# mLSTM cell and SwiGLU block on one core: another order of engines and transfers ahead of the first hidden block

## The chip, the core and the metric

The kernel runs on one core of one Trainium2 chip. The metric is the device time of one execution in microseconds. The times are medians of several executions of the same program; single executions of it lie between 551.8 and 552.71 us.

## What is computed

The reference is an mLSTM cell over 4 batches, 8 heads, 768 steps and a head size of 40, then a gated feed-forward block over the 3072 resulting tokens of width 320, with 1536 hidden features.

```python
for t in range(S):
    m_new = np.maximum(f_gate[:, :, t] + m, i_gate[:, :, t])
    f_stab = np.exp(f_gate[:, :, t] + m - m_new)
    i_stab = np.exp(i_gate[:, :, t] - m_new)
    m = m_new
    C = f_stab * C + i_stab * outer(vt, kt)
    n = f_stab * n + i_stab * kt
    denom = np.maximum(np.abs(n . qt), 1.0)
    y[:, :, t] = sigmoid(o_gate[:, :, t]) * (C @ qt) / denom
x = y.transpose(0, 2, 1, 3).reshape(3072, 320)
g = x @ w_gate
out = (g * sigmoid(g) * (x @ w_val)) @ w_out
```

## The kernel before, in words

The sequence is cut into six chunks g of 128 steps; a chunk holds the same 128 steps of all four batches, that is 512 tokens. For each chunk the cell is computed in matrix form (scores of q and k, weighed by decays, times v, plus the contribution of the state), and the result is turned so that features lie on partitions (xT). The feed-forward block of the chunk follows: `hidden(g, m)` makes one of 12 blocks of 128 hidden features with 20 matmuls (L651, gate rows on the partitions 0 to 63 and value rows on 64 to 127, side by side), a Silu (L656) and a product (L657); `project` multiplies the 12 blocks with w_out (L667, L674). While the block of chunk g runs on PE, the cell of chunk g + 1 is put between its matmuls by hand-written tables (`slots`, `after`, `ahead`). The schedule is manual: every engine does its instructions in the order in which the code emits them, and waits are added where data or rooms need them.

Before the first `hidden` nothing can be put between, so the first chunk has functions of its own (`first_...`), in an order written out by hand at the end of that part. In that order:

- `first_mask`, `first_inputs`, `first_maxima` and `first_exp` make the decay weights W0 of the first chunk, which lie in `h_sb[:, 0:8]`, the room that later holds hidden blocks. Each batch u has two of the eight places.
- `first_turn(P, ...)` turns k and q of two batches (P is 0 for batches 0 and 1, and 1 for 2 and 3) with whole 128x128 transposes (L509) and copies the results. `turn_one` (L296), which later chunks use, does it with 64-row pieces, two side by side.
- `first_scores(P)` multiplies k and q (L519) and puts the products into W0 (L523, DVE). `first_own(u)` multiplies W0 with v (L530), which reads W0 of batch u. `first_x(u)` divides (L535 to L538, DVE). `first_gate(P)` multiplies with the sigmoid of o_gate (L544, DVE) and copies 64 columns (L545, POOL). `sig(P)` is that sigmoid (L463, ACT).
- `first_seam(P, engs)` turns x to xT (L564) and copies it with the three named engines. `first_state(P)` makes the state (L552), `first_kept` copies it.
- `burn(n)` is n matmuls of no use, which keep PE busy.

The weights come as 8-byte floats. `piece_load(p)` asks for a piece (L165): for gate and value weights two transfers, gate rows to partitions 0 to 63 on SP's queue, value rows to 64 to 127 on ACT's queue for the first pieces and on SP's for later ones; for w_out one transfer on SP's queue. A piece lands in a room of its own (`raw`, two in turn) or in a tile that is still free (`home`: parts of `h_sb`, `wo_sb`). Then `scale(j)` splits block j on ACT (L190 the upper words, L192 the lower), `join(j)` shifts and masks the upper words on DVE (L199, L200), and `rounded(j)` adds the lower ones (L207, on POOL, or on DVE where the code names it). `convert` is the three together. Piece 0 holds block 0, piece 1 block 1, pieces 2 to 6 two blocks each, pieces 7 to 9 w_out.

ACT and SP ask for transfers in the same order in which their other instructions stand. A transfer request that must wait for a room holds everything behind it on that engine. SP has no other work: it asks for k, q and v of both P (L117), then o_gate of P = 0, o_gate of P = 1, and then the gate halves.

PSUM has eight banks in two groups of four, "cell" and "gen"; `bank(name, tag)` takes the next of its group in turn and waits until what it held was read.

Of the kernel before, what the change touches and what calls it, by code (L numbers as in the profile page):

```python
# [19 lines left out]
SUB = 64  # L20
# [4 lines left out]
def kernel(  # L25
# [112 lines left out]
    PIECES = [("gv", 0, 1), ("gv", 1, 1)] + [("gv", m, 2) for m in range(2, NFC, 2)] + [("o", m, 4) for m in range(0, NFC, 4)]  # L138

    def piece_load(p, home=None):  # L140
        kind, m, n = PIECES[p]
        if kind == "gv":
            a, d = NKC, n * 128
            src = [(slice(i * HP, (i + 1) * HP), w[:, m * 128:(m + n) * 128].rearrange("(c p) f -> p c f", p=HP))
                   for i, w in enumerate((moe_w_gate, moe_w_val))]
            queues = (nc.sync, nc.scalar if p < 5 else nc.sync)
        else:
            a, d = n, DM
            src = [(slice(0, 128), moe_w_out[m * 128:(m + n) * 128].rearrange("(a p) d -> p a d", p=128))]
            queues = (nc.sync,)  # L150
# [8 lines left out]
        if home is None:  # L159
            raw = conv.tile([128, 4 * NKC * 128], U32, name="raw")  # L160
        else:
            raw = home.rearrange("p a t -> p (a t)").bitcast(U32)
# [22 lines left out]
    def scale(j):  # L185
        if j in blocks:
            lo, hi, dst = blocks[j]
            a, d = hi.shape[1], hi.shape[2]
            top = conv.tile([128, NKC * 128], F32, name="top", bufs=1).rearrange("p (a d) -> p a d", a=a)
            nc.scalar.mul(top, hi.bitcast(F32), 2.0 ** -112)  # L190
            low = conv.tile([128, NKC * 128], I32, name="low").rearrange("p (a d) -> p a d", a=a)
            nc.scalar.mul(low, lo, 2.0 ** -29)  # L192
            blocks[j] = (low, top.bitcast(U32), dst)
# [97 lines left out]
    def turn_one(P, src, dst, engs):  # L291
        tp = [bank("tp_kq").rearrange("p (a t) -> p a t", t=SUB) for _ in range(2)]
        for a in range(UA):
            h = P * UH + 2 * a
            for i in range(2):
                nc.tensor.transpose(tp[i][:, a, :], src[half(i), h:h + 2, :].rearrange("p h d -> p (h d)"),  # L296
                                    ident[half(i), half(i)])
        for i in range(2):
            copy(engs[i], dst[:, P * UA:(P + 1) * UA, half(i)], tp[i])
# [128 lines left out]
    def xT(n):  # L428
        return xTs[max(n - 1, 0) % 2]
# [44 lines left out]
    A, V, G = nc.scalar, nc.vector, nc.gpsimd  # L474
    HH = H // 2
# [65 lines left out]
    def first_gate(P):  # L541
        for u in (2 * P, 2 * P + 1):
            x = x_sb[:, u, 0:DM].rearrange("p (h d) -> p h d", d=D)
            nc.vector.tensor_tensor(x, x, o_sb[:, u * H:(u + 1) * H], op=ALU.mult)  # L544
# [13 lines left out]
    def first_seam(P, engs):  # L558
        for c, eng in zip(range(0, NKC, 2), engs):
# [5 lines left out]
            copy(eng, xT(0)[:, c:c + len(cs), 2 * P * L:(2 * P + 2) * L].rearrange("p c (u s) -> p c u s", u=2), tp)  # L565

# [13 lines left out]
    first_turn(1, k_sb, kT, (A, A))  # L580
    first_x(0)
    first_turn(1, q_sb, qT, (A, V))
    load(o_sb, o_gate, 0, 1)
    piece_load(0)
# [5 lines left out]
    piece_load(1)  # L590
    burn(3)
    first_own(2)
    piece_load(2, h_sb[:, 1:1 + NKC])
# [3 lines left out]
    first_gate(0)  # L597
    first_x(2)
    first_x(3)
    first_gate(1)  # L600
    first_seam(0, (A, A, V))
    scale(0)
    ps1 = first_state(1, "gen")
    burn(1, "gen")
    piece_load(3, h_sb[:, NH - NKC:])
    join(0)
    first_seam(1, (A, A, V))
    rounded(0, V)
    first_kept(0, first_state(0), A)
    first_kept(1, ps1, V)  # L610
    convert(1, V)
    nc.scalar.activation(warm, warm, AF.Silu)
    piece_load(4, wo_sb)
    piece_load(5)

# [104 lines left out]
    def load_all(dst, a, n):  # L720
        for P in range(2):
            load(dst, a, n, P)

    run = lambda f, *a, **b: (lambda: f(*a, **b))
# [9 lines left out]
        1: [run(piece_load, 6), run(late_decay)],  # L734
# [4 lines left out]
        6: [run(turn, 1, (A, A), (A, V)), run(piece_load, 7)],  # L739
        7: [run(weights_sub, 1, 0), run(weights_mask, 0), run(weights_sub, 1, 1), run(weights_mask, 1), run(nc.gpsimd.memset, q_sb, 0.0)],  # L740
        8: [run(weights_exp, 0), run(weights_exp, 1), run(weigh_values, G, 0), run(weigh_values, G, 1),
            run(piece_load, 8)],
        9: [run(do_scores), run(do_weigh, 0), run(do_weigh, 1), run(do_decayed, 2), run(load_all, o_sb, o_gate, 1)],
        10: [run(do_add, 1), run(do_state, 2), run(rounded, 12), run(load_squares, q_sq, q, 2, (0,))],
        11: [run(do_attend, 1, 0), run(do_gather, 1, 0, False), run(piece_load, 9),
# [107 lines left out]
```

## Time and profile before

| what | value |
|---|---|
| median of three runs | 551.9 us (551.8 to 552.71) |
| the profiled execution's own time | 551.99 us |
| its span, from first to last instruction | 550.0 us |
| PE busy | 544.9 us |
| DVE busy | 236.1 us |
| ACT busy | 136.1 us |
| POOL busy | 103.0 us |
| HBM read | 35.68 MB |
| granted PE clock | 1.00 throughout |

A line of the timeline gives the start in us from the span's start, the duration in us, the engine (a q behind it means that the engine's sequencer asks for a transfer), the line of the kernel, the operation, the tiles written and read, and how many instructions were merged; in brackets stands the idle time before it and what ended it. A line of the chain gives start, duration, engine, tile and line of that piece of the chain that ended last. A line of the transfers gives the tiles, the queue, the number of requests, their size and the median time from request to landing. Times in words of the text are us from the span's start.

### The profile page before, as it was taken

What the parts mean: (1) busy time and instruction counts of PE and PEld (TensorE: products, weight loads), DVE (VectorE), ACT (ScalarE), POOL (GpSimd) and SP (SyncE); (2) the same over time, 40 slices, a digit from 0 to 9 for tenths busy, and PEclk for the clock granted to TensorE, in tenths of its full rate; (3) what the DMA queues carried; (4) which work ended last, traced back from release to release, by engine and by line L of the source; (5) the groups of instructions that cost most, each with busy time, mean ns of one, the idle gap of its engine ahead of it and who ended that gap; (6) DMA issues with size and microseconds to landing.
All of it is one profiled execution on the core that took longest, in us unless ns stands there. A gap on an engine that the chain in (4) does not pass through costs nothing.

```text
span 550.0 us, 11592 instructions
## 1 busy us (share of the span) xinstructions
PE 544.9 (99%) x4989; PEld 311.4 (57%) x4989; DVE 236.1 (43%) x397; ACT 136.1 (25%) x203; POOL 103.0 (19%) x95
## 2 busy tenths in 40 slices
PE   8999999999999999999999999999999999999997
PEld 4964556774555575545575545576455567444475
DVE  5778668961346232455421545531436621111100
ACT  4376755352110133011024101115110100111100
POOL 2304265673011060011133011124001100000000
PEclk9999999999999999999999999999999999999999
DMA  9999997878431762660564551395000131000000
GB/s 123 177 294 184 188 277 154 146 104 118 53 49 23 120 112 64 74 74 11 87 117 104 63 72 14 59 146 113 1 1 2 32 63 40 12 1 0 2 24 24
DMA packets 223994, 45.69 MB, mean 83 GB/s; under 512 B 214504, under 2 KB 219112, under 8 KB 223944
## 3 DMA queue, kind: packets, MB, share of 16 engines
q1 hardware_dynamic: 222036, 42.11, 46.7%
q10 hardware_dynamic: 1908, 2.85, 1.9%
q8 instruction: 39, 0.64, 0.5%
q14 instruction: 11, 0.09, 0.1%
HBM read 35.68 MB, written 4.01 MB: 72 GB/s over the span
## 4 chain that ended last, share of the span: by engine, by line
PE 98%; DVE 1%; ACT 0%; issue 0%; ACTq 0%; DVEq 0%
PE gv_ps L651 57%; PE o_ps L667 24%; PE o_ps L674 5%; PE inter L377 2%; PE sp L331 2%; PE intra L382 2%; PE add L353 1%; PE first_y L530 1%; PE burn L469 1%; PE tp_kq L509 1%; PE sp L519 1%; PE wps L480 0%; PE tp_kq L296 0%; PE wps L484 0%; PE wps L489 0%; PE tp_x L439 0%
## 5 line engine op out<-in xcount | busy, mean ns | idle before, releaser
L651 PE MATMUL gv_ps<-xT,wgv_sb 64*128 64x512 f32 x1440 | 316.6, 593 | 0.3 <-DVE wgv_sb L207 0.3
L651 PEld LDWEIGHTS gv_ps<-xT,wgv_sb 64*128 64x128 f32 x1440 | 138.1, 187 | 159.1 <-issue 156.4
L657 DVE TENSOR_TENSOR h_sb<-sg,gv_ps 128x512 f32<-128x512 f32 x72 | 49.5, 688 | 212.3 <-ACT sg L656 212.3
L667 PE MATMUL o_ps<-wo_sb,h_sb 128*128 128x320 f32 x480 | 130.5, 433 | 0.0
L667 PEld LDWEIGHTS o_ps<-wo_sb,h_sb 128*128 128x128 f32 x480 | 90.8, 190 | 41.0 <-issue 3.8
L656 ACT ACTIVATE sg<-gv_ps 128x512 f32<-128x512 f32 x72 | 43.0, 597 | 263.7 <-PE gv_ps L651 263.7
L456 POOL TENSOR_SCALAR_AFFINE_SELECT w_sb<-w_sb 64x1024 f32<-64x1024 f32 x20 | 28.5, 1423 | 63.9 <-DVE w_sb L451 62.9
L362 POOL TENSOR_TENSOR C<-C,dec 128x328 f32<-128x328 f32 x20 | 14.5, 738 | 134.8 <-DVE C L369 134.8
L661 ACT COPY z_sb<-o_ps 128x320 f32<-128x320 f32 x24 | 10.0, 423 | 93.2 <-PE o_ps L667 89.4
L403 POOL TENSOR_TENSOR o_sb<-o_sb,y_sb 128x640 f32<-128x640 f32 x10 | 14.2, 1431 | 78.9 <-DVE y_sb L394 78.9
L674 PE MATMUL o_ps<-wo_sb,h_sb 128*128 128x320 f32 x96 | 26.9, 437 | 0.0
L451 DVE TENSOR_TENSOR w_sb<-g_T,w_sb 128x1024 f32<-128x1024 f32 x10 | 13.1, 1354 | 28.6 <-DMA w_sb<-M_dram 28.6
L426 DVE STREAM_TRANSPOSE xT<-x_sq 128x640 f32<-128x640 f32 x16 | 12.5, 822 | 22.9 <-DMA x_sq<-x_sb 22.9
L674 PEld LDWEIGHTS o_ps<-wo_sb,h_sb 128*128 128x128 f32 x96 | 17.9, 190 | 7.2
L394 DVE TENSOR_TENSOR y_sb<-y_sb,intra 64x328 f32<-64x328 f32 x40 | 19.7, 492 | 0.7
L369 DVE TENSOR_TENSOR C<-C,add 40x328 f32<-40x328 f32 (+1 forms) x36 | 17.7, 493 | 1.2 <-POOL C L362 0.6
L377 PEld LDWEIGHTS inter<-C,qT 64*64 64x64 f32 x640 | 10.2, 134 | 7.3 <-issue 6.1
L460 ACT ACTIVATE w_sb<-w_sb 128x1024 f32<-128x1024 f32 x10 | 10.6, 1058 | 12.7 <-POOL w_sb L456 12.7
L207 POOL TENSOR_TENSOR wgv_sb<-wgv_sb,low 128x640 int32<-128x640 int32 x6 | 9.3, 1546 | 23.5 <-DVE wgv_sb L200 23.5
L341 POOL TENSOR_TENSOR vw_sb<-v_sb,w_sb 128x656 f32<-128x656 f32 x10 | 12.8, 1306 | 0.4
L338 DVE TENSOR_TENSOR w_sb<-sp,w_sb 128x512 f32<-128x512 f32 x20 | 12.7, 682 | 0.0
L397 DVE TENSOR_SCALAR den<-den 128x16 f32<-128x16 f32 x10 | 12.2, 1215 | 0.3
(132 smaller groups left out, 344.5 us busy)
## 6 DMA issues: line engine op xcount, KB each, us to landing
w_sb<-M_dram SPq DMA_DIRECT2D x10, 512.0 KB, 7.3
x_sq<-x_sb SPq DMA_DIRECT2D x128, 40.0 KB, 2.0
k_sb<-in_k_dram SPq DMA_DIRECT2D x12, 320.0 KB, 6.0
v_sb<-in_v_dram SPq DMA_DIRECT2D x12, 320.0 KB, 5.6
o_sb<-in_o_gate_dram SPq DMA_DIRECT2D x12, 320.0 KB, 5.5
raw<-in_moe_w_out_dram SPq DMA_DIRECT2D x3, 1280.0 KB, 7.5
out_dram<-z_sb SPq DMA_DIRECT2D x24, 160.0 KB, 1.8
q_sb<-in_q_dram SPq DMA_DIRECT2D x32, 64.0 KB, 2.3
```

The source lines that it names most:

```text
L362: nc.gpsimd.tensor_tensor(state(s + 1)[:, a], state(s)[:, a], dec[:, s - 2, a].unsqueeze(2).to_broadcast([128, UA, D1]), op=ALU.mult)
L369: nc.vector.tensor_tensor(c, c, ps[r], op=ALU.add)
L377: nc.tensor.matmul(inter[two][half(i), a, :], lhsT=qT[half(two), P * UA + a, half(i)], rhs=state(2 * n + i)[half(two), P * UA + a, :], sta ...
L394: nc.vector.tensor_tensor(t, t, intra[i][half(c)], op=ALU.add)
L403: eng.tensor_tensor(o, o, y[:, :, 0:D], op=ALU.mult)
L451: nc.vector.tensor_tensor(w_sb[:, heads(P)], gb, w_sb[:, heads(P)], op=ALU.subtract)
L456: nc.gpsimd.affine_select(w, w, compare_op=ALU.is_ge, fill=NEG, base=0, pattern=[[0, UH], [1, SUB]], channel_multiplier=-1)
L651: nc.tensor.matmul(ps[i], lhsT=wgv_sb[half(i), m, PAIRS[kc][i] if g < 2 else kc, :], rhs=x[half(i), kc, :], start=(kc == 0), stop=(kc == N ...
L656: nc.scalar.activation(sg, ps[0], AF.Silu)
L657: nc.vector.tensor_tensor(hid(g, m), sg, ps[1], op=ALU.mult)
L667: nc.tensor.matmul(p, lhsT=hid(g, m)[:, ts(u, L)], rhs=wo_sb[:, m, :], start=(m == 0), stop=(m == NFC - 1))
L674: nc.tensor.matmul(ps[u], lhsT=hid(g, m)[:, ts(u, L)], rhs=wo_sb[:, m, :], start=(m == 0), stop=(m == NFC - 1))
```

## The change

The change touches only the part ahead of the first `hidden`, the list of pieces, and the slots in which later pieces are asked for.

- Pieces: blocks 0 to 3 become one piece each, blocks 4 to 11 pairs; so pieces are numbered one higher from there on. Value halves go on ACT's queue up to piece 5 instead of up to piece 4.
- Rooms: piece 2 (block 2) lands in `h_sb[:, 2:5]`, piece 3 (block 3) in `h_sb[:, 8:11]`, piece 4 in `wo_sb`, piece 7 in `h_sb[:, 8:13]`.
- The second turn of k and q is done by `turn_one`, k's in "gen" banks, and `first_x(0)` stands behind both turns instead of between them.
- Piece 0 is asked for ahead of the second half of o_gate, piece 1 behind it; pieces 2 and 3 directly one behind the other ahead of `sig(1)`.
- `scale(0)` and `join(0)` move ahead of `sig(1)` and behind `first_x(2)`; `rounded(0, V)` moves ahead of `first_seam(1)`.
- `first_gate(0)` is done by POOL. One `burn` of three goes.
- `scale(1)` stands ahead of `first_kept(0)`; `join(1)` and `rounded(1, V)` behind `first_kept(1)`.
- `scale` is written as two functions; `first_seam` gets an argument `between` that stays empty.

```diff
--- before.py
+++ after.py
@@ -135,7 +135,7 @@
 
 
     raws = {}
-    PIECES = [("gv", 0, 1), ("gv", 1, 1)] + [("gv", m, 2) for m in range(2, NFC, 2)] + [("o", m, 4) for m in range(0, NFC, 4)]
+    PIECES = [("gv", m, 1) for m in range(4)] + [("gv", m, 2) for m in range(4, NFC, 2)] + [("o", m, 4) for m in range(0, NFC, 4)]
 
     def piece_load(p, home=None):
         kind, m, n = PIECES[p]
@@ -143,7 +143,7 @@
             a, d = NKC, n * 128
             src = [(slice(i * HP, (i + 1) * HP), w[:, m * 128:(m + n) * 128].rearrange("(c p) f -> p c f", p=HP))
                    for i, w in enumerate((moe_w_gate, moe_w_val))]
-            queues = (nc.sync, nc.scalar if p < 5 else nc.sync)
+            queues = (nc.sync, nc.scalar if p < 6 else nc.sync)
         else:
             a, d = n, DM
             src = [(slice(0, 128), moe_w_out[m * 128:(m + n) * 128].rearrange("(a p) d -> p a d", p=128))]
@@ -159,7 +159,7 @@
         if home is None:
             raw = conv.tile([128, 4 * NKC * 128], U32, name="raw")
         else:
-            raw = home.rearrange("p a t -> p (a t)").bitcast(U32)
+            raw = flat(home).bitcast(U32)
         raw = raw[:, 0:2 * a * d]
         for (r, w), queue in zip(src, queues):
             queue.dma_start(out=raw[r].rearrange("p (a d) -> p a d", a=a), in_=w.bitcast(U32))
@@ -182,15 +182,25 @@
                 for c in range(0, n, 2):
                     blocks[NFC + (m + c) // 2] = (lo[:, c:c + 2], hi[:, c:c + 2], wo_sb[:, m + c:m + c + 2, :])
 
-    def scale(j):
+    def scale_top(j):
         if j in blocks:
             lo, hi, dst = blocks[j]
             a, d = hi.shape[1], hi.shape[2]
             top = conv.tile([128, NKC * 128], F32, name="top", bufs=1).rearrange("p (a d) -> p a d", a=a)
             nc.scalar.mul(top, hi.bitcast(F32), 2.0 ** -112)
+            blocks[j] = (lo, top.bitcast(U32), dst)
+
+    def scale_low(j):
+        if j in blocks:
+            lo, *rest = blocks[j]
+            a, d = lo.shape[1], lo.shape[2]
             low = conv.tile([128, NKC * 128], I32, name="low").rearrange("p (a d) -> p a d", a=a)
             nc.scalar.mul(low, lo, 2.0 ** -29)
-            blocks[j] = (low, top.bitcast(U32), dst)
+            blocks[j] = (low, *rest)
+
+    def scale(j):
+        scale_top(j)
+        scale_low(j)
 
     def join(j):
         if j in blocks:
@@ -288,8 +298,8 @@
     M_dram = tc.dram_tile([BH, S - L], F32, name="M_dram")
 
 
-    def turn_one(P, src, dst, engs):
-        tp = [bank("tp_kq").rearrange("p (a t) -> p a t", t=SUB) for _ in range(2)]
+    def turn_one(P, src, dst, engs, tag="cell"):
+        tp = [bank("tp_kq", tag).rearrange("p (a t) -> p a t", t=SUB) for _ in range(2)]
         for a in range(UA):
             h = P * UH + 2 * a
             for i in range(2):
@@ -472,6 +482,7 @@
         return slice(u * BH, (u + 1) * BH)
 
     A, V, G = nc.scalar, nc.vector, nc.gpsimd
+    run = lambda f, *a, **b: (lambda: f(*a, **b))
     HH = H // 2
     wps = {}
 
@@ -538,10 +549,10 @@
         nc.vector.tensor_tensor(x_sb[:, u, 0:DM].rearrange("p (h d) -> p h d", d=D), y[:, :, 0:D],
                                 den.to_broadcast([128, H, D]), op=ALU.mult)
 
-    def first_gate(P):
+    def first_gate(P, eng):
         for u in (2 * P, 2 * P + 1):
             x = x_sb[:, u, 0:DM].rearrange("p (h d) -> p h d", d=D)
-            nc.vector.tensor_tensor(x, x, o_sb[:, u * H:(u + 1) * H], op=ALU.mult)
+            eng.tensor_tensor(x, x, o_sb[:, u * H:(u + 1) * H], op=ALU.mult)
         nc.gpsimd.tensor_copy(x_sb[:, 2 * P:2 * P + 2, DM:], x_sb[:, 2 * P:2 * P + 2, 0:HP])
 
     def first_state(P, tag="cell"):
@@ -555,7 +566,7 @@
     def first_kept(P, ps, eng):
         copy(eng, state(2)[:, P * UA:(P + 1) * UA], ps)
 
-    def first_seam(P, engs):
+    def first_seam(P, engs, between={}):
         for c, eng in zip(range(0, NKC, 2), engs):
             cs = range(c, min(c + 2, NKC))
             tp = bank("tp_x")[:, 0:len(cs) * 2 * L].rearrange("p (c u s) -> p c u s", u=2, s=L)
@@ -563,6 +574,8 @@
                 for b in range(2):
                     nc.tensor.transpose(tp[:, w - c, b, :], x_sb[:, 2 * P + b, ds(PAIRS[w][0] * HP, 2 * HP)], ident)
             copy(eng, xT(0)[:, c:c + len(cs), 2 * P * L:(2 * P + 2) * L].rearrange("p c (u s) -> p c u s", u=2), tp)
+            for f in between.get(c, ()):
+                f()
 
     burn(7)
     banks = [(u, j) for j in range(2) for u in range(B)]
@@ -577,41 +590,45 @@
     first_scores(0)
     first_own(0)
     late_sums()
-    first_turn(1, k_sb, kT, (A, A))
+    turn_one(1, k_sb, kT, (A, A), "gen")
+    turn_one(1, q_sb, qT, (A, V))
     first_x(0)
-    first_turn(1, q_sb, qT, (A, V))
+    piece_load(0)
     load(o_sb, o_gate, 0, 1)
-    piece_load(0)
+    piece_load(1)
     first_own(1)
     first_values(1)
     first_scores(1)
     first_x(1)
     sig(0)
-    piece_load(1)
-    burn(3)
+    burn(2)
     first_own(2)
-    piece_load(2, h_sb[:, 1:1 + NKC])
+    piece_load(2, h_sb[:, 2:5])
+    piece_load(3, h_sb[:, NH - NKC:NH - 2])
+    first_x(2)
+    scale(0)
+    join(0)
     sig(1)
     burn(2)
     first_own(3)
-    first_gate(0)
-    first_x(2)
+    first_gate(0, G)
     first_x(3)
-    first_gate(1)
+    first_gate(1, V)
     first_seam(0, (A, A, V))
-    scale(0)
     ps1 = first_state(1, "gen")
     burn(1, "gen")
-    piece_load(3, h_sb[:, NH - NKC:])
-    join(0)
+    rounded(0, V)
     first_seam(1, (A, A, V))
-    rounded(0, V)
-    first_kept(0, first_state(0), A)
+    ps0 = first_state(0)
+    piece_load(4, wo_sb)
+    scale(1)
+    first_kept(0, ps0, A)
     first_kept(1, ps1, V)
-    convert(1, V)
+    join(1)
+    rounded(1, V)
     nc.scalar.activation(warm, warm, AF.Silu)
-    piece_load(4, wo_sb)
     piece_load(5)
+    piece_load(6)
 
 
     pair = early.tile([BH, PP], F32)
@@ -721,7 +738,6 @@
         for P in range(2):
             load(dst, a, n, P)
 
-    run = lambda f, *a, **b: (lambda: f(*a, **b))
 
 
     on_vector = (9, 10, 11)
@@ -731,18 +747,18 @@
     slots = {
         0: [run(convert, 2, V), run(late_maxima), run(load_all, k_sb, k, 1),
             run(nc.sync.dma_start, out=M_dram, in_=flat(M_sb)), run(load_all, q_sb, q, 1)],
-        1: [run(piece_load, 6), run(late_decay)],
+        1: [run(piece_load, 7, h_sb[:, NH - NKC:]), run(late_decay)],
         2: [run(nc.scalar.activation, step1, step1, AF.Exp), run(decay_rows), run(weights_load, 1), run(load_all, v_sb, v, 1)],
         3: [run(late_turns)],
         4: [run(decay)],
         5: [run(turn, 0, (A, A), (A, V))],
-        6: [run(turn, 1, (A, A), (A, V)), run(piece_load, 7)],
+        6: [run(turn, 1, (A, A), (A, V)), run(piece_load, 8)],
         7: [run(weights_sub, 1, 0), run(weights_mask, 0), run(weights_sub, 1, 1), run(weights_mask, 1), run(nc.gpsimd.memset, q_sb, 0.0)],
         8: [run(weights_exp, 0), run(weights_exp, 1), run(weigh_values, G, 0), run(weigh_values, G, 1),
-            run(piece_load, 8)],
+            run(piece_load, 9)],
         9: [run(do_scores), run(do_weigh, 0), run(do_weigh, 1), run(do_decayed, 2), run(load_all, o_sb, o_gate, 1)],
         10: [run(do_add, 1), run(do_state, 2), run(rounded, 12), run(load_squares, q_sq, q, 2, (0,))],
-        11: [run(do_attend, 1, 0), run(do_gather, 1, 0, False), run(piece_load, 9),
+        11: [run(do_attend, 1, 0), run(do_gather, 1, 0, False), run(piece_load, 10),
              run(load_squares, q_sq, q, 2, (1,))],
     }
     for m in range(NFC):
```

## The prediction

> **What bounds the kernel now.** I read the page first: engines, then the chain that ended last, then that chain in order of time for the first 33 us, and last the transfers.
>
> ```profile
> PE 544.9 (99%) x4989; PEld 311.4 (57%) x4989; DVE 236.1 (43%) x397; ACT 136.1 (25%) x203; POOL 103.0 (19%) x95
> PE 98%; DVE 1%; ACT 0%; issue 0%; ACTq 0%; DVEq 0%
> ```
>
> PE is the chain for 98% of the span. From 32.04 us, where the first gate/value matmul (gv_ps, L651) starts, PE runs without a gap to the last copy. No edit changes PE's work behind that point, so the question is when gv_ps starts. The chain ahead of it:
>
> ```profile
> 16.80 0.90 PE tp_kq L509 x8
> ...
> 17.73 1.06 PE tp_kq L509 x8
> ...
> 22.49 0.76 PE burn L469 x3
> ...
> 25.39 1.73 PE first_y L530 x16
> ...
> 27.78 0.49 DVE x_sb L538
> 28.27 0.80 DVE x_sb L544 x2
> ...
> 31.08 0.83 DVE wgv_sb L207
> 31.91 0.14 issue
> ```
>
> Two engines are full here. PE works from 15.04 to 31.76 and then waits 0.28 us for the rounding of weight block 0 (L207). DVE has no pause from 21.70 (products of the second scores) to 31.91. Behind both stand the transfers, from the timeline and two transfer answers (issue, KB, us from issue to landing):
>
> ```profile
> 14.44 4.94 SPq L117 DMA_DIRECT2D o_sb<-in_o_gate_dram  x2
> 18.40 0.68 ACTq L165 DMA_DIRECT2D raw<-in_moe_w_val_dram  x1
> 25.72 0.74 ACT L463 ACTIVATE o_sb<-o_sb 128x640 f32<-128x640 f32 x1 [3.61 <-DMA raw<-in_moe_w_val_dram]
> 28.57 0.83 ACT L190 ACTIVATE top<-raw 128x640 f32<-128x640 f32 x1
> ```
> ```profile
> raw<-in_moe_w_gate_dram SPq DMA_DIRECT2D x1, 320.0 KB, 8.8
> ```
>
> The gate half of piece 0, asked at 19.43, lands at 28.2; the split of block 0 (L190, 28.57) cannot come sooner. The first half of o_gate (asked 14.44, 6.9 us) lands at 21.34, the second (16.83, 8.2 us) at 25.0.
>
> **The Trainium skill.** (1) "SBUF — State Buffer", section "Door 1: The DMA port swizzle": 64 partitions reach half of the ports. Gate weights go to partitions 0 to 63, value weights to 64 to 127. The trace agrees: with gate weights alone from 26 to 30 us it moved 198 GB/s. The same page's "Can I just issue two DMAs to hit both halves?" says no; here the trace differs, 360 GB/s from 36 to 40 us with gate on SP's queue and value on ACT's. (2) "DMA: Bandwidth & Descriptors", section "Queues, rings and completion order": an engine takes turns between queues. The trace agrees: from 20 to 21 us ACT's queue moved 236 packets and SP's, full of o_gate, 62. (3) "TensorE: Matmul & The Clock Gate", section "Why this matters for your kernels": no PE gaps above about 3 us, or the clock halves. This trace has no such gap; mine below is under 1 us. (4) "SBUF — State Buffer", section "Who interferes with whom": GpSimd and a two-port DVE instruction shut each other out. The trace agrees: L199 took 1.14 us at 58.53 beside a POOL add, against 0.49.
>
> **Part by part.**
>
> *Turns of k and q, second pair.* first_turn's 16 whole transposes (0.90 + 1.06 us) become turn_one's 32 small ones; the same 32 (L296) stand later in the chain at 0.99 us. PE saves 0.97. One *burn* of three goes: 0.76 / 3 = 0.25. With the 0.28 wait, PE's own floor is 32.04 - 0.97 - 0.25 - 0.28 = 30.54. The banks rotate otherwise (k's turn takes two "gen" banks); every bank was read at least 1 us before, the nearest being scores(1), whose last two banks are q's: copied by ACT at about 19.2, needed at 20.5. first_x(0) now stands behind q's copy on DVE, ends near 19.8 instead of 18.6, and its bank is wanted at 22.0: free.
>
> *DVE.* Scores start at 20.51 - 0.97 = 19.54, products at 20.73, end about 23.2. Then first_x(1) and first_x(2) at 1.12 each: 25.3. first_gate(0) leaves DVE (0.88) for POOL: two multiplies at half of L403's 1431 ns for twice the width, 0.72 each, and the 0.29 copy. POOL is idle; the first runs from about 22.2 and the second after first_x(1), so all is done by 25.5, and seam(0) asks at about 25.9. Were POOL twice as slow, that would cost up to 1 us before seam(0), mostly inside the later wait for seam(1). Then, new in this place, join(0): 1.34 (29.43 to 30.78 before), first_x(3) 1.13, first_gate(1) 0.88. From gate(1) to gv_ps PE needs seam(1) and first_state(0): 29.45 to 31.76 before, 2.31 plus 0.06 for the handover. rounded(0) (0.83) and both xT copies fit beside that. So gv_ps = J + 1.34 + 1.13 + 0.88 + 2.37 = J + 5.7, where J is join(0)'s start. With J = 25.3: 31.0. PE then idles at most 0.9 us before seam(1).
>
> *ACT.* The new order is value DMA of piece 2, of piece 3, scale(0), sig(1). Piece 2's DMA waits for first_own(2), which still reads its room: for its first two heads (about 22.5) or all (23.7). Behind it wait piece 3's DMA, both scales and sig(1). On SP, piece 3 and 4 stand behind piece 2 too; nothing in them is needed before 44 us. Each DMA seems to wait for the one eight before it (SP's piece 4 was asked at 28.29, as piece 0's gate half landed), so piece 3's value DMA waits for that half. If it lands at p, scale's top is done at p + 0.63 (DMA issue) + 0.83 + 0.1, so J = p + 1.6 and gv_ps = p + 7.3. Up to p = 23.7 this costs nothing beyond J = 25.3. Before, scale(0) stood behind the seam copies; now join(0) blocks DVE if p is late.
>
> *Transfers.* On SP piece 0's gate goes before the second half of o_gate. The first half still lands at 21.34. Each half piece is 328 KB: 1.65 us at 198 GB/s alone, 0.9 if gate and value pair at 360. So p = 21.34 + (1.8 to 3.3), plus up to 0.3 for larger packets: 23.1 to 24.9; I take 24.0, which gives gv_ps 31.3. The second half of o_gate lands at L = p + 328 / 151 = 2.17 (151 GB/s from 16 to 20 us) + what piece 1's value half takes in between, 0 to 1.65: 25.3 to 28.7; I take 27.0. Then sig(1) 0.74, gate(1) 0.88, handovers 0.1 and 2.37: gv_ps = L + 4.1 = 31.1.
>
> *Pieces behind.* Block 1 is needed one block (4.35 us) later, about 35.7; piece 1 lands by 30, scale, join, rounding as before (3.1 us) from 31: done by 34.2. The same bytes of weights for blocks 2 to 9 are asked at similar times; k and q of the next chunk follow them. q's first half landed at 56.0 for a transpose at 60.0, so 4 us of slippage there are free. Piece 7's room in h_sb is split before hid(0,8) is written. Piece 5's value half moves to ACT's queue: 0.6 us of issue on ACT, which sat idle 1.48 us before the first Silu (L656, 36.60). scale in two functions issues the same instructions. Cost taken: 0; if the cover fails, the turn of k or q waits for what exceeds 4 us.
>
> *Sum.* gv_ps at 31.3 by p, 31.1 by L, 31.0 by DVE, 30.54 by PE. The latest counts; with 0.1 for handovers, 31.4, that is 0.64 us earlier. The profiled run: span 550.0, 551.99 with what lies around it; less 0.64, 551.35. It stands 0.09 above the median of 551.9, so I forecast 551.3. A difference of 0.2% (1.1 us) is about what can be told from no change.
>
> **Rivals.**
> *Nothing late (faster).* p below 23.7, L below 26.9, and DVE a few tenths quicker: gv_ps 30.54 to 30.93, up to 1.5 us gained; 550.6. For it: PE and DVE both lose work. Against: DVE's own sum says 31.0.
> *A wash.* No pairing: p = 24.9, L = 28.7. gv_ps = 32.2 by p, 32.8 by L, a loss up to 0.8: 552.7. For it: packets of gate weights ran alone from 25 to 31 us although value weights were asked at 25.04.
> *The o_gate half is crowded out (slower).* sig(1) now waits for a transfer behind three half pieces, and by turns perhaps a fourth (piece 2's value, asked by 22.5). At 1.65 each, L = 21.34 + 4 x 1.65 + 2.17 = 30.1, gv_ps 34.2, lost 2.2: 554.1. It decides from L = 27.9; 0.2% are lost from L = 29.0. For it: this half landed at 25.0, only 0.7 before its use. Against: one queue's turn seldom holds more than one of its transfers here.
>
> **How the numbers follow.** Forecast (gv_ps 30.94 to 31.75) 0.45; wash (to 33.1) 0.23; nothing late 0.12; crowded out 0.20. Faster by over 0.2%: 0.12. Within: 0.45 + 0.23 = 0.68. Slower: 0.20. The range of 550.7 to 553.2 leaves out about 0.05 below and 0.15 above.
>
> **What would show it.** L296 in place of L509 at 16.8 us, at about 1.0; products at 20.7; first_gate(0) on POOL at 0.72 each; the top of scale(0) at about 25 to 26; sig(1) ending by 27.9; gv_ps at 31.4, then the same 515 us of PE. Wrong it would be if sig(1) starts after 28, if join(0) starts after 26.5, or if PE waits anywhere behind gv_ps.

## The result, and the profile after

The changed kernel takes 556.15 us (median; single executions 554.58 to 558.27) against 551.9: a ratio of 1.0074, 95% interval 1.0056 to 1.0092. It is slower, outside the range of the forecast and on its other side. The profiled execution took 555.98 us, span 553.7, against 551.99 and 550.0: 3.99 us to account for.

First the page of the kernel after: the engines, and the chain that ended last.

```profile
PE 546.6 (99%) x5003; PEld 310.4 (56%) x5004; DVE 235.2 (42%) x395; ACT 135.8 (25%) x203; POOL 104.6 (19%) x97
PE 86%; DMA 5%; SPq 4%; issue 2%; POOL 1%; ACT 1%; DVE 1%; ACTq 0%; POOLq 0%; DVEq 0%
```

PE still looks 99% busy. The second line gives it away: before, PE was 98% of the chain and no transfer was in it; now transfers and SP's requests are 9%. In order of time, these transfers and what follows them (start, duration, what):

```profile
19.98 13.75 DMA raw<-in_moe_w_gate_dram
37.09 13.15 PE gv_ps L668 x60
...
60.49 11.83 DMA w_sb<-M_dram
72.36 3.88 issue
76.27 2.07 POOL w_sb L466
```

So PE was held twice: by the gate half of piece 1, asked at 19.98 and landed at 33.73, and by the decays of the next chunk (w_sb). PE's timeline over that stretch:

```profile
31.95 4.56 PE L668 MATMUL gv_ps<-xT,wgv_sb 64*128 64x512 f32 x20
37.09 13.15 PE L668 MATMUL gv_ps<-xT,wgv_sb 64*128 64x512 f32 x60 [0.58 <-DVE wgv_sb L217]
50.90 4.56 PE L668 MATMUL gv_ps<-xT,wgv_sb 64*128 64x512 f32 x20
...
81.62 5.60 PE L668 MATMUL gv_ps<-xT,wgv_sb 64*128 64x512 f32 x20
87.40 0.31 PE L363 MATMUL add<-vw_sb,k_sb 64*64 64x41 f32 x2 [0.17 <-DVE w_sb L348]
87.99 2.33 PE L363 MATMUL add<-vw_sb,k_sb 64*64 64x41 f32 x126 [0.29 <-DVE w_sb L348]
90.26 1.13 PE L668 MATMUL gv_ps<-xT,wgv_sb 64*128 64x512 f32 x4
...
101.37 0.89 PE L392 MATMUL intra<-v_sb,w_sb 64*64 64x41 f32 x43 [0.78 <-issue]
```

The same points stood before at 32.04, 50.22, 87.45 and 98.75 (the last is the first `o_ps` behind the products, L382 before and L392 after; after at 102.19). Before, PE ran through the add without a wait:

```profile
85.44 2.08 PE L353 MATMUL add<-vw_sb,k_sb 64*64 64x41 f32 x128
87.45 4.56 PE L651 MATMUL gv_ps<-xT,wgv_sb 64*128 64x512 f32 x20
```

Differences between the points give the account:

| stretch | after less before, us |
|---|---|
| start of the first gate/value matmul (31.95 against 32.04) | -0.09 |
| blocks 0 to 3: the wait for block 1 (50.90 against 50.22, less -0.09) | +0.77 |
| to behind the add L363 (90.26 against 87.45, less 0.68) | +2.13 |
| to the first o_ps behind L392: the gap called "issue" (3.44 less 2.81) | +0.63 |
| rest of the span, and what lies around it (0.26 + 0.29) | +0.55 |
| sum | +3.99 |

The front gave nothing, and over half of the loss arose at the add, 50 us behind it. How a late transfer gets there is read from SP's requests (the number after the start is how long the request held SP). After:

```profile
19.98 5.41 SPq L165 DMA_DIRECT2D raw<-in_moe_w_gate_dram  x1
25.52 1.26 SPq L165 DMA_DIRECT2D h_sb<-in_moe_w_gate_dram  x2
...
37.25 16.45 SPq L117 DMA_DIRECT2D k_sb<-in_k_dram  x2
53.80 1.43 SPq L485 DMA_DIRECT2D M_dram<-M_sb  x1
...
57.78 1.94 SPq L165 DMA_DIRECT2D h_sb<-in_moe_w_gate_dram  x1
...
60.49 9.22 SPq L457 DMA_DIRECT2D w_sb<-M_dram  x2
```

Before:

```profile
33.20 16.15 SPq L117 DMA_DIRECT2D k_sb<-in_k_dram  x2
49.44 1.31 SPq L724 DMA_DIRECT2D M_dram<-M_sb  x1
...
53.38 2.00 SPq L165 DMA_DIRECT2D raw<-in_moe_w_gate_dram  x1
...
56.13 8.59 SPq L447 DMA_DIRECT2D w_sb<-M_dram  x2
```

k has two requests, one for each half, and each k line shows both. The second, asked at 37.04 before and at 37.67 after, holds SP until 49.34 before and until 53.70 after, while the weights ahead of it in SP's queue move. All behind it is 4.4 us late. What that meets, from the timelines of ACT, DVE and POOL after:

```profile
70.24 0.79 ACT L190 ACTIVATE top<-h_sb 128x640 f32<-128x640 f32 x1 [2.40 <-DMA h_sb<-in_moe_w_val_dram]
71.06 0.49 DVE L209 TENSOR_SCALAR wgv_sb<-top 128x640 uint32<-128x640 uint32 x1 [3.35 <-ACT top L190]
74.97 2.36 DVE L461 TENSOR_TENSOR w_sb<-g_T,w_sb 128x1024 f32<-128x1024 f32 x2 [1.00 <-DMA w_sb<-M_dram]
76.27 6.75 POOL L466 TENSOR_SCALAR_AFFINE_SELECT w_sb<-w_sb 64x1024 f32<-64x1024 f32 x4 [13.37 <-DVE w_sb L461]
83.06 1.06 ACT L470 ACTIVATE w_sb<-w_sb 128x1024 f32<-128x1024 f32 x1 [2.29 <-POOL w_sb L466]
86.66 2.48 DVE L348 TENSOR_TENSOR w_sb<-sp,w_sb 128x512 f32<-128x512 f32 x4
```

ACT waits 2.40 us for the value half of piece 7, which holds DVE; then DVE waits 1.00 for w_sb. Before, DVE came to this subtraction without a wait, at 71.68:

```profile
71.68 2.35 DVE L451 TENSOR_TENSOR w_sb<-g_T,w_sb 128x1024 f32<-128x1024 f32 x2
```

From there the work is in series: subtraction (L461), masks on POOL (6.75 us), exp on ACT, products (L348), the add on PE. ACT's Silu of the running block stands behind that exp, so PE is held by its own block as well (5.60 us in place of 4.56).

Why was piece 1's gate half late? SP's request for it started at 19.98, but held SP for 5.41 us and ended only at 25.39. By then ACT's two requests for the values of pieces 2 and 3 had ended, at 23.84 and 25.05:

```profile
23.23 1.82 ACTq L165 DMA_DIRECT2D h_sb<-in_moe_w_val_dram  x2
```

Packets that moved from 26.8 to 29.1 us, by queue (q1 is SP's, q10 ACT's; number, MB, time as a share), after:

```profile
DMA packets 437, 0.44 MB, mean 191 GB/s; under 512 B 15, under 2 KB 436, under 8 KB 436
...
q10 hardware_dynamic: 436, 0.43, 108.2%
```

and before:

```profile
DMA packets 363, 0.45 MB, mean 195 GB/s; under 512 B 20, under 2 KB 273, under 8 KB 362
...
q1 hardware_dynamic: 362, 0.44, 111.0%
```

After, ACT's queue had these 2.3 us to itself, with the value halves of pieces 2 and 3; before, SP's queue with gate halves. In the trace SP's queue pauses from 26.76 to 29.18 after, and never over 0.4 us from 24.4 to 50 before. The bill comes next. Four-us windows of the kernel after and of the kernel before (length, PE busy, granted clock, share of the DMA engines, GB/s):

```profile
28.00:32.00 4.00, 3.71 (x73) 1.00 1.13 200
32.00:36.00 4.00, 4.00 (x22) 1.00 1.11 198
36.00:40.00 4.00, 3.42 (x18) 1.00 1.07 209
```
```profile
28.00:32.00 4.00, 3.76 (x78) 1.00 1.06 197
32.00:36.00 4.00, 3.96 (x19) 1.00 1.05 315
36.00:40.00 4.00, 4.00 (x22) 1.00 1.05 360
```

Before, gate and value halves go side by side from 32 us at 315 to 360 GB/s. After, values went alone, and then gates alone, each at about 200.

### The profile page after: what moved, and what is told of

The parts are those of the page before. It is cut to its first block, busy times and chain, and to the rows that moved or that the text cites. A ratio compares the mean times of both kernels' runs of the same rounds, so it can differ in the third digit from the quotient of the medians.

```text
span 553.7 us, 11627 instructions
## 1 busy us (share of the span) xinstructions
PE 546.6 (99%) x5003; PEld 310.4 (56%) x5004; DVE 235.2 (42%) x395; ACT 135.8 (25%) x203; POOL 104.6 (19%) x97
## 4 chain that ended last, share of the span: by engine, by line
PE 86%; DMA 5%; SPq 4%; issue 2%; POOL 1%; ACT 1%; DVE 1%; ACTq 0%; POOLq 0%; DVEq 0%
PE gv_ps L668 51%; PE o_ps L684 24%; PE o_ps L691 5%; SPq L117 3%; DMA raw<-in_moe_w_gate_dram 2%; DMA w_sb<-M_dram 2%; PE inter L387 2%; PE intra L392 2%; PE sp L341 1%; PE add L363 1%; POOL w_sb L466 1%; SPq L165 1%; DVE w_sb L348 0%; ACT top L190 0%; PE tp_x L449 0%
## 5 line engine op out<-in xcount | busy, mean ns | idle before, releaser
L461 DVE TENSOR_TENSOR w_sb<-g_T,w_sb 128x1024 f32<-128x1024 f32 x10 | 13.1, 1356 | 27.3 <-DMA w_sb<-M_dram 27.3
L190 ACT ACTIVATE top<-raw 128x640 f32<-128x640 f32 x12 | 9.6, 800 | 16.5 <-DMA raw<-in_moe_w_gate_dram 5.9
L348 DVE TENSOR_TENSOR w_sb<-sp,w_sb 128x512 f32<-128x512 f32 x20 | 12.7, 682 | 0.0
```

## The experiments

Theories as named in the expectations. T, sharpened later to Q and R: piece 1's gate half is overtaken by later value halves on ACT's queue (whose turn it is: R), and everything behind it in SP's queue is late (Q). A: two transfers more for blocks 2 and 3 are the cost. B: the edits on PE, DVE and POOL. C: in the first four runs, the second o_gate half behind piece 0; from the fifth run on, C is the granted clock.

One number serves all runs: the *stretch*, from the start of the first gate/value matmul to the first one behind the add. It has the 220 matmuls of 11 blocks and the next chunk's scores in it, and took 55.41 before and 58.31 after; it tells the loss behind the front apart from the front.

**1. Values of pieces 2 and 3 later**

```diff
-    piece_load(2, h_sb[:, 2:5])
-    piece_load(3, h_sb[:, NH - NKC:NH - 2])
     first_x(2)
     scale(0)
     join(0)
     sig(1)
+    piece_load(2, h_sb[:, 2:5])
+    piece_load(3, h_sb[:, NH - NKC:NH - 2])
```

> The changed kernel, with the requests for pieces 2 and 3 moved behind sig(1): on ACT their value halves are asked for at about 28 us instead of 23.2 and 24.5; SP's order stays. Theory (piece 1's gate half lands late, at 33.7, because value halves of later pieces go ahead of it, and everything behind it on SP is late with it): its gate half lands at about 29.5, PE does not wait for block 1, the next chunk's k, q and decays come about 4 us sooner, 552 us. Rival A (blocks 2 and 3 as pieces of their own cost two more requests, each of which holds a later one): 556. Rival B (POOL's gate, small turns, other banks): 556. Rival C (o_gate's second half behind piece 0): 556.

Measured: 554.63 us (552.69 to 555.34), ratio 1.0045 (1.0032 to 1.0057). The first half of T came: piece 1's gate half landed at 30.49 and block 1 did not wait. The time did not: ACT reached the two requests only at 27.86, behind sig(1), which waits for the second half of o_gate (landed at 27.78), and block 2 waited instead.

```profile
42.20 9.21 PE L668 MATMUL gv_ps<-xT,wgv_sb 64*128 64x512 f32 x40 [1.56 <-DVE wgv_sb L217]
```

The lateness moved on by one block.

**2. The pieces and rooms alone, in the kernel before**

```diff
-    PIECES = [("gv", 0, 1), ("gv", 1, 1)] + [("gv", m, 2) for m in range(2, NFC, 2)] + ...
+    PIECES = [("gv", m, 1) for m in range(4)] + [("gv", m, 2) for m in range(4, NFC, 2)] + ...
...
-    piece_load(2, h_sb[:, 1:1 + NKC])
+    piece_load(2, h_sb[:, 2:5])
+    piece_load(3, h_sb[:, NH - NKC:NH - 2])
```

> The kernel before with the new pieces and rooms alone (blocks 2 and 3 singly, both asked for behind first_own(2), later pieces one number higher); the order of engines, piece 0 behind o_gate and piece 1 behind sig(0) stay. Theory: piece 1's gate half is asked for at 22.3, before any value half of pieces 2 and 3, and lands at about 30 as before: 552 within 1. Rival A: 555 to 556. Rivals B and C: 552.

Measured: 552.75 us (552.14 to 553.94), ratio 1.0010 (1.0001 to 1.0019). Stretch 55.38, piece 1's gate half at 28.21. A falls: four transfers for blocks 2 and 3 in place of two cost at most 0.19%.

**3. The engines alone, in the kernel before**

```diff
-    first_turn(1, k_sb, kT, (A, A))
+    turn_one(1, k_sb, kT, (A, A), "gen")
+    turn_one(1, q_sb, qT, (A, V))
     first_x(0)
-    first_turn(1, q_sb, qT, (A, V))
...
-    burn(3)
+    burn(2)
...
-    first_gate(0)
+    first_gate(0, G)
```

> The kernel before with the engine edits alone: turn_one for the second pair, first_gate(0) on POOL, one burn less; pieces, rooms and the order of all transfers stay. Theory: the first gv_ps still waits for block 0, whose gate half lands at 28.2, so nothing is won or lost: 551.9 within 0.5. Rival B: 555 to 556. Rivals A and C: 552.

Measured: 552.47 us, ratio 1.0022 (1.0007 to 1.0036). The median hides two groups: 14 executions from 551.42 to 553.27 with a mean granted clock of 0.999 or 1.0, and six from 554.94 to 556.59 with 0.990 to 0.994. The profiled execution is of the upper group. PE's timeline, then the windows:

```profile
16.59 0.71 PE L296 MATMUL tp_kq<-ident,k_sb 64*128 64x64 f32 x16
17.64 0.83 PE L296 MATMUL tp_kq<-ident,q_sb 64*128 64x64 f32 x16 [0.34 <-DMA q_sb<-in_q_dram]
18.40 3.63 PE L530 MATMUL first_y<-v_sb,h_sb 128*128 128x41 f32 x16
```
```profile
14.00:18.00 4.00, 3.50 (x51) 1.00 1.35 143
18.00:22.00 4.00, 4.00 (x30) 0.51 1.04 185
22.00:26.00 4.00, 4.00 (x38) 0.64 1.25 200
```

PE now reaches q's turn before q's second half has landed and waits 0.34 us; in 14 to 18 us it is busy for 3.50 us (3.81 before), and the clock then halves until about 25 us. The 16 matmuls at 18.40 take 3.63 us instead of 1.88, and gv_ps starts at 34.99. The stretch is 55.37. So there is a second cost in the change, about 3 us (median of the six 555.45, of the fourteen 552.4) in some executions, and none in the rest. The profile of the kernel after does not have it; two of its five executions have a mean clock of 0.991 and 0.993 and are its longest, 557.61 and 558.27.

**4. The second o_gate half ahead of piece 0**

```diff
-    piece_load(0)
     load(o_sb, o_gate, 0, 1)
+    piece_load(0)
     piece_load(1)
```

> The changed kernel with the second half of o_gate asked for ahead of piece 0 again; all else as changed. Theory: piece 0's gate half then lands at about 28 and piece 1's no sooner than 33; join(0) holds DVE until 29, first_x(3) and first_gate(1) behind it, so gv_ps starts at about 34: 557 or more. Rival C: 552. Rivals A and B: 556.

Measured: 556.25 us (555.28 to 558.33), ratio 1.0080 (1.0055 to 1.0105). C's 552 did not come. But the profile shows other losses than the kernel after has: piece 1's gate half landed at 29.18, the stretch is 55.38, and the clock is at 0.50 from 18 to 27 us, so that ACT asks for pieces 2 and 3 only at 27.81 and gv_ps starts at 36.24. One of the four executions kept a mean clock of 1.0 and still took 555.51. So the total alone does not settle C, and a total that agrees with a theory is no proof of its mechanism; kernel 7, which has the new order alone, decides it.

**5. Piece 6's value half on ACT's queue**

```diff
-            queues = (nc.sync, nc.scalar if p < 6 else nc.sync)
+            queues = (nc.sync, nc.scalar if p < 7 else nc.sync)
```

> The changed kernel with one edit: piece 6's value half is asked on ACT's queue and not on SP's. Theory Q (SP's queue loses 4 us at piece 1's gate half, and k, M_dram and w_sb stand behind it): one 640 KB transfer less lies ahead of k's second half on SP, so M_dram and w_sb are asked 3 to 4 us earlier, w_sb lands by 72 (74.87 after), the masks follow at once and the add is unstalled, about 2 us long; piece 1 still lands at 33.7 and costs 0.7. Time 553.5, between 552.7 and 554.5. Rival K (the add is late through work on ACT or DVE that is itself late, not through w_sb): w_sb may land early, but exp and add stay where they are, 556.

Measured: 553.25 us (552.13 to 557.44), ratio 1.0032 (1.0015 to 1.0049), as Q has it. But in the profiled execution piece 1's gate half landed at 29.71, with the same front, so block 1 did not wait either, and Q needed a stricter test (10). What differed: ACT asked for piece 0's value half at 18.86, not at 18.32.

**6. Only the turns of k and q as before**

```diff
-    turn_one(1, k_sb, kT, (A, A), "gen")
-    turn_one(1, q_sb, qT, (A, V))
+    first_turn(1, k_sb, kT, (A, A))
     first_x(0)
+    first_turn(1, q_sb, qT, (A, V))
```

> The changed kernel with one edit: k's and q's second turns are again four and four 128x128 transposes on either side of first_x(0), in place of two calls of turn_one. Theory C (the shorter turns make PE wait for q's second half at 17.3 to 17.6, and in part of the runs the granted clock halves for 7 to 10 us afterwards): the runs above 556.5 disappear, the rest stay at 554.5 to 556.5, median 555.5. Rival (the upper runs have another cause): runs of 557 to 558 stay.

Measured: 555.28 us, ratio 1.0045 (1.0028 to 1.0063). No execution above 556.32, all seven with a clock of 1.0. That the runs above 556.5 are gone is weak evidence for C, with five executions of the kernel after and seven of this one. They fall into two groups, 552.94 to 553.35 (three, which neither theory had) and 555.28 to 556.32 (four). The profiled one is of the upper group, with piece 1's gate half at 33.01, a wait of 0.39 at block 1 and a stretch of 57.98: the loss of the kernel after without its clock.

**7. The order of requests alone, in the kernel before**

```diff
-    load(o_sb, o_gate, 0, 1)
     piece_load(0)
+    load(o_sb, o_gate, 0, 1)
+    piece_load(1)
...
     sig(0)
-    piece_load(1)
     burn(3)
```

> The kernel before with the new order of requests in front alone: piece 0, second o_gate half, piece 1; pieces in pairs from block 2 on, engines and bursts as before. Theory Q: the order alone is enough, since piece 1's value half and the first pair's value half go on ACT's queue while SP's is held by the o_gate half; piece 1's gate half lands at 32 or later, SP's queue is 3 us or more behind, w_sb lands at 73 or later: 554.5, between 553.5 and 556. Rival A' (order and the finer pieces are needed together): piece 1 lands by 30.5, and the time is 552.3.

Measured: 553.12 us (552.0 to 559.43, 22 executions), ratio 1.0022 (1.0009 to 1.0036). Q missed: piece 1's gate half landed at 29.18, stretch 55.38. Here the first later value half is asked at 25.56, not at 23.23. The order is not enough, which also leaves C no more than the 0.36% of this run's interval; the early requests of pieces 2 and 3 belong to it. A' came nearer, though 553.12 is above its 552.3.

**8. The second o_gate half on GpSimd's queue**

```diff
-    load(o_sb, o_gate, 0, 1)
+    nc.gpsimd.dma_start(out=o_sb[:, heads(1), 0:D], in_=tokens(o_gate, 0, 1))
```

> The changed kernel with one edit: the second o_gate half is asked on GpSimd's queue instead of SP's. Theory Q: SP asks piece 1's gate half right behind piece 0's and it lands by 29, SP's queue has 2048 small packets less ahead of k, M_dram and w_sb, which land no later than in the kernel before, the add is unstalled; the second o_gate half lands at 27 to 28.5 as before, so the first gate and value matmul starts at 31 to 32.3. Time 551.4, between 550.4 and 552.6. Rival (POOL's own issuing or the small packets' turn on a third queue is late): o_gate lands at 30 or later, and the time is 553 or more.

Measured: 555.15 us (553.9 to 557.33), ratio 1.0060 (1.0042 to 1.0078). Half right: piece 1's gate half landed at 26.42 and the stretch is 55.40. But the o_gate half, asked by POOL at 19.97, landed at 29.78, about where the rival had it, and PE waited for its gate:

```profile
31.21 1.54 PE L575 MATMUL tp_x<-ident,x_sb 128*128 128x128 f32 x10 [1.92 <-DVE x_sb L555]
```

**9 and 10. All three requests earlier, without and with piece 6's value half on ACT's queue**

```diff
+    piece_load(0)
+    load(o_sb, o_gate, 0, 1)
+    piece_load(1)
     first_turn(1, k_sb, kT, (A, A))
     first_x(0)
     first_turn(1, q_sb, qT, (A, V))
-    piece_load(0)
-    load(o_sb, o_gate, 0, 1)
-    piece_load(1)
```

The diff is against kernel 6; the second of the two has the edit of kernel 5 as well.

> The changed kernel with k's and q's second turns again as before, and the three requests (piece 0, second o_gate half, piece 1) moved ahead of these turns. SP's order stays; ACT asks the value halves of pieces 0 and 1 some 2 to 3 us earlier. Theory R (whose turn it is: the queues take turns by transfer, and when ACT asks by about 18.4 its value halves are always one turn ahead of SP's gate halves): piece 1's gate half lands at 33 or later in every run, block 1 is late and w_sb lands at 74 or later; all runs at 554.8 to 557, none at 553 (the same kernel with the later requests had three runs at 552.9 to 553.4 beside four at 555.3 to 556.3). Rival (the two groups have nothing to do with the turns): two groups again.

> As the kernel with the requests ahead of the turns, and piece 6's value half on ACT's queue. Theory Q (SP's queue behind piece 1): piece 1 still lands at 33 and costs about 0.5 to 0.8, but w_sb lands by 72.5 and the add is about 2 us long: 553.5, between 552.8 and 554.3. Rival K (the add is late for another reason): 555.5 or more.

Measured: 558.98 us (558.31 to 559.31, ratio 1.0122, 1.0109 to 1.0135) and 557.5 us (555.25 to 558.96, ratio 1.0097, 1.0079 to 1.0114). The first total is above every expectation, and the second lies where K put it (555.5 or more). In both the o_gate half came late too: SP asked for it only at 24.34 and 24.99, behind requests that had held SP for about 5 us each, and it landed at 31.25 and 31.74, so that gv_ps starts at 35.21 and 37.24. As R says, piece 1's gate half is last, 36.23 and 36.76. It costs no wait at block 1, since block 0 is as late; what remains is SP's queue, so the pair tests Q by the stretch and not by the total. PE's timeline around the add, first kernel 9:

```profile
90.31 0.31 PE L363 MATMUL add<-vw_sb,k_sb 64*64 64x41 f32 x2 [0.17 <-DVE w_sb L348]
90.91 2.33 PE L363 MATMUL add<-vw_sb,k_sb 64*64 64x41 f32 x126 [0.29 <-DVE w_sb L348]
93.17 4.56 PE L668 MATMUL gv_ps<-xT,wgv_sb 64*128 64x512 f32 x20
```

and kernel 10, with one 640 KB transfer less on SP's queue:

```profile
90.62 2.08 PE L363 MATMUL add<-vw_sb,k_sb 64*64 64x41 f32 x128
92.62 4.56 PE L668 MATMUL gv_ps<-xT,wgv_sb 64*128 64x512 f32 x20
```

The stretch goes from 57.96 to 55.38, that is 2.58 us, and w_sb lands 42.58 us after the start of gv_ps in the one and 37.50 in the other. Of these 5.08 us, 3.05 are the earlier landing (77.79 and 74.74); the rest is the later start of gv_ps, which also makes room. DVE needs w_sb about 39.6 us after that start, and with the start of kernel 9 it would have landed at 39.5, so the edit alone just suffices. Kernels 5 and 11 say the same: w_sb at 39.29 and 39.32, no wait, and stretches of 55.58 and 55.40, against 42.93 and 58.31 in the kernel after and 42.59 and 57.98 in 6. Q stands, K falls.

**11 and 12. Piece 1 behind first_own(2), without and with piece 6's value half on ACT's queue**

```diff
     piece_load(0)
     load(o_sb, o_gate, 0, 1)
-    piece_load(1)
...
     first_own(2)
-    piece_load(2, h_sb[:, 2:5])
-    piece_load(3, h_sb[:, NH - NKC:NH - 2])
+    piece_load(1)
     first_x(2)
     scale(0)
     join(0)
+    piece_load(2, h_sb[:, 2:5])
+    piece_load(3, h_sb[:, NH - NKC:NH - 2])
```

Again against kernel 6; the second has the edit of kernel 5 as well.

> The changed kernel with k's and q's second turns as before, piece 1 asked behind first_own(2), and pieces 2 and 3 behind scale(0) and join(0). Theory R: nothing stands between piece 0 and the second o_gate half, which lands at 27 to 27.4; the first gate and value matmul starts at 31.1 to 31.7; piece 1's halves move side by side and land by 30.5, w_sb by 73: 551.9, between 551.2 and 552.8. Rival (any value half on ACT is ahead of SP's, wherever it is asked, and lateness only moves to block 2 or 3): a wait of 0.5 to 1.6 at block 1, 2 or 3, and 553.5 or more.

> As the kernel with piece 1 behind first_own(2), and piece 6's value half on ACT's queue. Theories Q and R: w_sb lands 1.5 to 3 us earlier than without this edit, which is worth something only if the add still waited there: 551.6, between 551.0 and 552.4. Rival: as for that kernel, 553 or more.

Measured: 553.39 us (551.73 to 556.41, ratio 1.0026, 1.0009 to 1.0043) and 552.59 us (551.85 to 557.04, ratio 1.0023, 1.0005 to 1.0040). In the first profile R's points come: the o_gate half at 26.04, gv_ps at 31.52, piece 1 at 29.17, stretch 55.40. Its time does not (551.2 to 552.8): 0.97 us of "issue" at L392 eat the gain of 0.5 at the front, and about 1.2 us more of a span of 551.6 (550.0 before) were not traced. In the second, ACT asked for piece 2's value half at 26.58, it landed at 39.25, and block 2 waited:

```profile
43.66 10.55 PE L668 MATMUL gv_ps<-xT,wgv_sb 64*128 64x512 f32 x40 [2.04 <-DVE wgv_sb L217]
```

The rival's lateness that moves on is therefore real in this execution (556.91), and likely in the two beside it (three of 15 at 556.8 to 557.04, twelve at 551.85 to 553.42). Neither beats the kernel before.

Side by side, from each kernel's profiled execution: when the requests for piece 0's two halves ended and when the halves landed, when SP's request for piece 1's gate half and ACT's first one for a later value half ended, when piece 1's gate half landed, and GB/s from 32 to 36 us. A request ends at its start plus the time that it held its engine.

| kernel | piece 0, ended: value, gate | landed: value, gate | piece 1 gate, ended | later value, ended | piece 1 gate landed | GB/s | stretch |
|---|---|---|---|---|---|---|---|
| after | 19.00, 19.09 | 22.86, 24.43 | 25.39 | 23.84 | 33.73 | 198 | 58.31 |
| 6 | 18.86, 19.11 | 22.37, 23.91 | 24.96 | 23.93 | 33.01 | 199 | 57.98 |
| 1 | 19.09, 19.23 | 22.79, 24.36 | 25.29 | 28.46 | 30.49 | 203 | 57.52 |
| 11 | 18.97, 19.14 | 22.51, 24.19 | 23.59 | 24.89 | 29.17 | 261 | 55.40 |
| 5 | 19.59, 19.10 | 24.45, 22.88 | 23.93 | 24.36 | 29.71 | 259 | 55.58 |
| 7 | 19.60, 18.66 | 25.56, 22.40 | 21.79 | 26.19 | 29.18 | 272 | 55.38 |
| 8 | 19.02, 18.88 | 24.33, 22.80 | 19.54 | 24.02 | 26.42 | 269 | 55.40 |
| 12 | 19.49, 18.75 | 26.39, 22.64 | 21.95 | 27.18 | 29.56 | 223 | 59.34 |

For these two pairs of transfers one rule fits every row: the one whose request ended first went first. So it was with the halves of piece 0, and piece 1's gate half was behind later values only where its own request ended behind theirs, in after and 6. The other six profiles agree; in 9 and 10 its request ended behind ACT's second one as well (27.37 behind 27.16, 28.16 behind 27.73), and it landed behind those values. With more transfers waiting on both queues they also moved side by side, as before from 32 us on. So in the kernel after, piece 1 was late because its request held SP for 5.41 us and ended 0.34 us behind ACT's second one. R looked at when ACT asks for piece 0; that does not decide piece 1, for in 1 and 11 the value half of piece 0 is first too, and piece 1 in time. No run varied the end of one request alone, so this rule is read from the traces and not tested. Kernel 5 has the front of the kernel after and fell on the other side.

## Why the prediction was wrong

**Failed: "Pieces behind".** It said that piece 1 lands by 30 and block 1 is done by 34.2. Piece 1's gate half landed at 33.73, and block 1 was done at 37.03. The step gave no working for this landing; it is the one of the kernel before (29.99). The new order let two value halves of later pieces through first, on the other queue. The prediction itself cites the Trainium skill, "DMA: Bandwidth & Descriptors", section "Queues, rings and completion order", that an engine takes turns between queues, and reckons with such turns only for the o_gate half (rival three, which had later values go ahead, but of the wrong victim: that half landed at 27.98, not 30.1). It set against this rival that a queue's turn seldom holds more than one of its transfers, though it says itself that gate weights ran alone from 25 to 31 us, several transfers in a row. Nor do these traces show the turns of the page: it lets an engine switch at each packet, and here 436 of 437 packets were of ACT's queue for 2.3 us, with SP's request ended 1.4 us earlier. The order of the requests' ends, in the table above, fits better.

**Failed: "4 us of slippage there are free".** It looked at q's transposes alone. In the same queue behind k stand piece 7's value half and w_sb. Before, the last pair's value half landed at 65.14 and was read at 67.03: 1.9 us of slack. For w_sb the trace before shows no landing of its second half, but kernel 11, whose DVE does not wait for it, has it 39.32 us after the start of gv_ps, where DVE reaches it at 39.6 (71.68 less 32.04 before): some 0.3 us. 4.4 us met these slacks, and the add came 2.13 later. Experiment 10 shows it by taking load off that queue, and kernel 5 agrees.

**Failed: "at similar times".** The gate halves of blocks 4 and 5 were asked at 28.00 (25.68 before), of 6 and 7 at 33.87 (28.29), of 8 and 9 at 35.40 (30.14), and k's first half at 37.25 (33.20). SP's request at 33.87 came right behind the landing of piece 1's gate half at 33.73, as the one at 30.14 before came behind its landing at 29.99: the prediction had noted that each DMA seems to wait for the one eight before, and did not carry it on to here. SP's queue had earlier pieces to move meanwhile (198 GB/s from 32 to 36 us), so how much of the 4.4 us is due to later requests and how much to slower transfers was not separated.

**Wrong, though not in the profiled execution: the clock.** The prediction cites the Trainium skill, "TensorE: Matmul & The Clock Gate", section "Why this matters for your kernels", that PE should have no gaps above about 3 us, and took shorter gaps as harmless. In kernel 3 the longest wait ahead of the drop is 0.34 us, and the clock halved all the same. The engine edits bring this: 6 of kernel 3's 20 executions have a mean clock of 0.997 or less, and none of the 34 of the kernel before beside them. Which of the three edits does it is open. The small transposes are not needed for a drop: over all runs, 18 of 55 executions with turn_one (after, 1, 3, 4, 5, 8) are that low, and of those without it 7 of 66 (2, 6, 7, 11, 12) and 9 of 10 (9 and 10, where PE waits longer). Nor does a low share of busy time suffice: from 14 to 18 us PE was busy for 3.50 us in kernel 3, for 3.58 in 1 and for 3.11 in 9, and the profiles of 1 and 9 keep the full clock there. In the kernel after itself no profile shows the drop.

**Right: the sums of the front.** L = 28.0 for the o_gate half plus 4.1 gives 32.1; measured 31.95. The same sum holds to 0.15 us in kernel 1 (27.78, 31.78), 5 (28.14, 32.10), 6 (27.44, 31.42), 8 (29.78, 33.74) and 9 (31.25, 35.21); in 10 the clock fell and gv_ps came 1.4 us behind it, and in 11 the o_gate half was too early to be what gv_ps waited for. The term that was mis-sized is L itself, taken as 27.0 and measured 27.98, inside the 25.3 to 28.7 that the prediction had for it. Piece 0's gate half (24.0 expected, 24.43), join(0) (25.6 expected, 25.93), and the two turns (0.99 expected, 1.14 from 17.08 to 18.22) came about as worked out; POOL's gate took 0.87 us each, not 0.72, and was in time.

**Open.** The 0.78 us called "issue" ahead of L392 is in the profiles of after, 4, 6, 9 and 11 (0.5 to 1.2 us) and in none of the others. It does not follow the late transfers (4 and 11 have it without them). The packets of queue q8, which the profile calls "instruction", give a likely cause: 39 packets with 0.64 MB are 64 bytes for each of PE's 10,007 matmuls and weight loads, so one packet holds about 256 of them. In all five profiles PE goes on 2.5 to 2.8 us after the start of such a packet (in the kernel after at 101.37, the packet at 98.83), and it stops 192 or 193 of them past a multiple of 256 (there 2240). So PE most likely waits for its own instructions. No run tests it, and why the packet comes too late in these five is open, as is whether the change brings the 0.63 us.

## What to carry to other kernels

When transfers are reordered, follow every queue past the change to the first reader that has no slack, and take the slack of each reader from the profile, not of the one that comes to mind. Where one piece is split over two queues, keep its halves level: half a piece that runs ahead gains nothing and takes the time of the half that somebody waits for. And if a step is made shorter so that its engine reaches the next transfer early, the gain is a wait, and in some executions of kernel 3 a lower clock came behind it.

## What the runs showed of the hardware

- Two queues that each write 64 partitions moved 315 to 360 GB/s together and about 200 with only one of them at work; the number of requests mattered little beside that (kernel 2).
- A request of 320 KB by SP took 5.41 us where 0.6 is usual, behind a half of o_gate with its small packets; SP asks for nothing else meanwhile.
- Of two transfers, one on SP's and one on ACT's queue, the one whose request ended first went first, for the two pairs compared in all 14 profiles: for piece 0, 0.09 us was enough (value 19.00 and gate 19.09 in the kernel after, value first; 19.59 and 19.10 in 5, gate first). Kernel 6 ran in two groups with medians 2.4 us apart; that this is why is likely, but only one of its groups was profiled.
- PE's granted clock fell to 0.50 for 7 to 10 us in kernels 3 and 4, though no wait of PE ahead of it was longer than 0.34 and 0.4 us.
- PE stood still for 0.5 to 1.2 us in five profiles, each time until 2.5 to 2.8 us after a packet of instructions had started to move; that it waited for them is likely.
